# Table loads on GpSimd's DMA queue, transposes behind the first loads, the inverse p matrix in its own tile, and tasks ordered by longest path

## The chip, the cores and the metric

The kernel runs on one core of one Trainium2 chip. Time is the device time of one execution in microseconds (us). All runs of one table row come from the same chip and are compared only with runs of the kernel before made beside them.

"Slow" is a run over 1.5% above the fastest of the same kernel; ratios use fast runs alone. A ratio is the mean time of one kernel's fast runs over that of the other's fast runs of the same rounds, so it is not quite the ratio of the medians quoted beside it, which cover all runs; its 95% interval stands in brackets. "Span" is the profiled execution, some 2 us shorter than the time of a whole run. Each kernel has one profile, and its positions carry a scatter that no edit made: the first eight 128x512 matmuls of branch B took 1.89 us in the profile of the kernel before and 3.12 to 3.55 in those of b4, b6, b7 and b8, whose edits lie behind them. So a position that differs by 2 or 3 us between two profiles shows nothing by itself; ratios of times rest on several runs.

## The reference, cut to what matters

```python
def _A_ref(x, w_r, w_i):                      # spectral filter, x: 1 x 2048 x 512
    X = rfft2(x.astype(float32), axes=(-2, -1))
    X = X * (w_r + 1j * w_i)                  # w: 2048 x 257, bf16
    return irfft2(X, s=(S, D), axes=(-2, -1)).astype(bfloat16)
def _B_ref(x, w1, b1, w2):                    # 512 -> 1792 -> 512
    h = x @ w1 + b1
    sp = log1p(exp(-abs(h))) + where(h > 0, h, 0)
    return (h * tanh(sp)) @ w2
g = sigmoid((x * gate_w).sum(-1, keepdims=True))
return g * _A_ref(x, A_w_r, A_w_i) + (1 - g) * _B_ref(x, B_w1, B_b1, B_w2)
```

## The kernel before: the parts that matter

The whole program is a graph of tasks. A list scheduler, run when the kernel is built, puts every task on an engine and fixes each engine's order; the engines then run their lists with semaphores. Some tasks may go to several engines, each with an estimated time and a bias. Branch B works in four chunks of 512 rows: first matrix (`mm1`), eviction with bias (`h`), exp, ln and tanh on ScalarE, a multiply (`mul`), second matrix (`mm2`). Branch A's filter tables are loaded, moved into place in 16 pieces of 32 x 2064, and half-copied: the real part as it is, the imaginary part negated.

```python
        def dve4(n): return 0.10 + n * 0.00027          # estimates of the scheduler
        def pool(n, k=2.15): return 0.12 + n * k * 0.001
        ...
        for ri, (src, nm) in enumerate(((A_w_r, "wr"), (A_w_i, "wi"))):
            ...                                         # ten table loads, SyncE's queue
                    ld(f"{nm}{fh}s{j}", sg[pm:32:2, fs, :], wv[:, ms, :], us, cls="d_w", writes=[(nm, fh, "s", j)])
        for t in range(xtp, NT):                        # eight DMA transposes of x, same queue
            ld(f"xt{t}", xT[:, t // 4, :, t % 4, :], xv[:, t, :], 0.64, cls="d_xt", transpose=True, writes=[("xT", t)])
        ...                                             # a table move, 32 x 2064
                            if pt == 0:
                                return e.tensor_copy(out=o_, in_=i_)
                            return e.tensor_scalar(out=o_, in0=i_, scalar1=1.0, scalar2=0.0, op0=ALU.mult, op1=ALU.add)
        ...                                             # the half copy, 64 x 4160; ri == 1: negated
                def f_dup(e, ri=ri, f0=f0, dstv=dstv):
                    if ri == 0:
                        return e.tensor_copy(out=dstv[64:128, f0:f0 + 32, :], in_=dstv[0:64, f0:f0 + 32, :])
                    return e.tensor_scalar(out=dstv[0:64, f0:f0 + 32, :], in0=dstv[64:128, f0:f0 + 32, :], scalar1=-1.0, scalar2=None, op0=ALU.mult)
                G.any(f"{nm}n{fh}", [("dve", dve4(4160), f_dup), ("pool", pool(4160, 0.95), f_dup, "b_dup")], "w", ..., writes=[wk])
        ...                                             # In (the filter's input) reuses the staging tile
            dma(f"s1r{g}", rE[g:128:4, 0:8192], scr_r[...], 1.5, reads=[("scr", g)], writes=[("In", g)], deps=t_mv)
```

The two imaginary half copies are called `win0` and `win1` below, the imaginary moves `wim...`, the evictions of the third chunk `h2_...`, multiplies `mul...`, one filter product `p2_0`. An eviction copies a result of the matrix engine (PE) out of PSUM. The matmul stages of branch A are p, d and t on the way in (their evictions: `ep`, `ed`, `et`), it and id on the way back; the inverse p matrix belongs to id. The gate is 64 small matmuls on the transposes of x; a gated output is branch B's result scaled by 1 - g. `deps=t_mv` says that the filter's input is read back only when all 16 moves are done.

## Time and profile before

| | before |
|---|---|
| time, median of 3 runs | 152.81 us (152.56 to 154.8) |
| span of the profiled run | 150.9 us |
| eight multiplies of the first chunk, VectorE | 13.0 us |
| wait of the gate for the transposes, matrix engine | 2.69 us |
| the "edge" (start of the first matmul behind the last filter add) | 105.55 us |
| span behind the edge | 45.4 us |

The prediction below shows the lines behind these. Two more are needed later: how the negations ran before. Here is their row in the groups of instructions (line, engine, operation, output<-input with shapes, count | busy us, mean ns of one | idle time before):

```profile
L757 DVE TENSOR_SCALAR rA<-rA 64x4160 bf16<-64x4160 bf16 x2 | 2.5, 1240 | 0.1
```

And these are lines of VectorE's work in order (start us, length us, engine, line, operation, and in brackets the idle time before and who ended it; `...` marks lines left out):

```profile
59.21 0.17 DVE L714 CAST ezb<-ez 128x16 bf16<-128x16 f32 x1 [0.28 <-ACT ez L713]
...
60.52 3.48 DVE L922 TENSOR_TENSOR rD<-ps,b1f 128x1024 bf16<-128x1024 f32 x3
...
74.75 1.29 DVE L948 TENSOR_TENSOR hs<-hs,uT 128x1024 bf16<-128x1024 bf16 x2 [1.28 <-ACT uT L939]
```

The negations run on VectorE in 1.24 us each. A 128x16 copy takes 0.17 us, three evictions 3.48 us, two multiplies 1.29 us.

### The profile page before, as it was taken

How to read it: one execution, taken by the hardware profiler on the slowest of the kernel's cores; microseconds unless marked ns; L12 is line 12 of the kernel's file. 1: busy time of each engine (PE TensorE's matmuls, PEld its weight loads, DVE VectorE, ACT ScalarE, POOL GpSimd, SP SyncE). 2: the span in 40 equal slices, each digit the busy share in tenths (PEclk: the TensorE clock that was granted, in tenths of full speed). 3: DMA queues.
4: the chain of work that ended last, by engine and by line, in shares of the span. 5: the costliest groups of instructions: out<-in, count | busy, mean ns of one | idle time of the engine just before them, and what ended most of it. 6: DMA issues, size and time to landing. Idle time of an engine off the chain costs nothing.

```text
span 150.9 us, 2300 instructions
## 1 busy us (share of the span) xinstructions
PE 134.9 (89%) x917; PEld 72.8 (48%) x917; DVE 128.6 (85%) x150; ACT 116.3 (77%) x77; POOL 45.7 (30%) x39
## 2 busy tenths in 40 slices
PE   5697999889957988999999999896799999999992
PEld 3455555454425323444456553342256667634471
DVE  0378996969999998989698999998869979999791
ACT  3549667699997733999999999998798999971111
POOL 3000059998977994001100005951000000000000
PEclk9999999999999599999999999999689999999999
DMA  5899999998848993998004765300000000000563
GB/s 130 278 361 379 166 181 145 321 343 150 189 102 177 304 297 67 371 412 343 4 0 110 168 146 147 69 0 0 0 0 0 4 0 0 0 4 0 208 230 120
DMA packets 22686, 22.37 MB, mean 148 GB/s; under 512 B 13524, under 2 KB 19540, under 8 KB 22228
## 3 DMA queue, kind: packets, MB, share of 16 engines
q1 hardware_dynamic: 22352, 22.00, 52.6%
q10 hardware_dynamic: 324, 0.23, 0.5%
q8 instruction: 7, 0.11, 0.4%
q14 instruction: 3, 0.02, 0.1%
HBM read 14.89 MB, written 4.19 MB: 126 GB/s over the span
## 4 chain that ended last, share of the span: by engine, by line
PE 69%; DVE 19%; DMA 6%; issue 2%; ACT 2%; SPq 1%; DVEq 0%
PE ps L964 30%; PE ps L915 26%; DVE hs L948 9%; DMA w_sb<-in_B_w_dram 4%; DVE hs L922 3%; PE ps L894 3%; PE ps L855 2%; PE ps L782 2%; DMA rE<-c_inv 2%; PE ps L990 2%; PE ps L688 2%; DVE rA L559 2%; DVE rB L663 1%; DVE rW L756 1%; PE ps L677 1%
## 5 line engine op out<-in xcount | busy, mean ns | idle before, releaser
L915 PE MATMUL ps<-rX,w_sb 128*128 128x512 bf16 x224 | 52.5, 388 | 1.7 <-DVE rE L880 0.8
L964 PE MATMUL ps<-w_sb,hs 128*128 128x512 bf16 (+1 forms) x182 | 39.5, 363 | 1.5 <-DMA w_sb<-in_B_w_dram 1.0
L915 PEld LDWEIGHTS ps<-rX,w_sb 128*128 128x128 bf16 x224 | 21.7, 100 | 27.5 <-issue 2.3
L922 DVE TENSOR_TENSOR hs<-ps,b1f 128x1024 bf16<-128x1024 f32 x21 | 25.3, 1217 | 3.4 <-PE ps L915 3.2
L964 PEld LDWEIGHTS ps<-w_sb,hs 128*128 128x128 bf16 x182 | 17.3, 98 | 19.9 <-DVE hs L948 2.4
L938 ACT ACTIVATE uT<-uT 128x4096 bf16<-128x4096 bf16 (+1 forms) x8 | 25.5, 3190 | 0.2
L939 ACT ACTIVATE uT<-uT 128x4096 bf16<-128x4096 bf16 (+1 forms) x8 | 25.5, 3188 | 0.1
L948 DVE TENSOR_TENSOR hs<-hs,uT 128x1024 bf16<-128x1024 bf16 (+1 forms) x24 | 22.0, 976 | 1.3 <-ACT uT L939 1.3
L936 ACT ACTIVATE uT<-hs 128x2048 bf16<-128x2048 bf16 (+1 forms) x12 | 20.3, 1691 | 3.2 <-DVE hs L948 2.1
L964 PE MATMUL ps<-w_sb,rD 128*128 128x512 bf16 x56 | 14.9, 414 | 1.0 <-DVE rD L948 1.0
L562 ACT ACTIVATE rC<-ps 128x1024 bf16<-128x1024 f32 x14 | 14.0, 1022 | 1.7 <-PE ps L677 1.7
L978 ACT ACTIVATE rX<-ps,omg 128x512 bf16<-128x512 f32 (+1 forms) x8 | 5.3, 660 | 11.1 <-PE ps L964 11.1
L744 POOL COPY rW<-rE 32x2064 bf16<-32x2064 bf16 x4 | 7.8, 1959 | 18.6 <-DMA rE<-in_A_w_r_dram 18.3
L663 DVE TENSOR_TENSOR rB<-rA 128x1024 bf16<-128x1024 bf16 (+2 forms) x10 | 6.6, 692 | 5.5 <-DMA rA<-in_A_x_dram 5.5
L559 DVE CAST rA<-ps 128x1024 bf16<-128x1024 f32 x7 | 8.6, 1294 | 1.1 <-PE ps L894 1.1
L796 POOL TENSOR_TENSOR rC<-rC,rW 128x1024 bf16<-128x1024 bf16 x2 | 4.0, 2025 | 18.0 <-DMA tmp<-rC 18.0
L559 DVE CAST rF<-ps 128x1024 bf16<-128x1024 f32 x8 | 9.1, 1216 | 0.4 <-PE ps L855 0.4
L744 POOL COPY rA<-rE 32x2064 bf16<-32x2064 bf16 x4 | 9.3, 2319 | 0.4 <-POOL rA L733 0.3
L994 DVE SCALAR_TENSOR_TENSOR rX<-ps,gcol,rX 128x512 bf16<-128x512 f32 x12 | 8.3, 745 | 1.2 <-PE ps L990 1.1
L964 PEld LDWEIGHTS ps<-w_sb,rD 128*128 128x128 bf16 x56 | 5.5, 104 | 7.1 <-issue 1.7
L922 DVE TENSOR_TENSOR rD<-ps,b1f 128x1024 bf16<-128x1024 f32 x7 | 8.3, 1218 | 0.7 <-PE ps L915 0.7
L981 DVE TENSOR_SCALAR rX<-ps,omg 128x512 bf16<-128x512 f32 (+1 forms) x9 | 6.5, 719 | 2.0 <-PE ps L964 1.8
(79 smaller groups left out, 160.8 us busy)
## 6 DMA issues: line engine op xcount, KB each, us to landing
rF<-c_m SPq DMA_DIRECT2D x1, 2048.0 KB, 12.7
scr<-rD SPq DMA_DIRECT2D x4, 512.0 KB, 7.4
rB<-c_g SPq DMA_DIRECT2D x1, 2048.0 KB, 7.9
rE<-scr SPq DMA_DIRECT2D x4, 512.0 KB, 9.8
tmp<-rC SPq DMA_DIRECT2D x16, 128.0 KB, 2.3
out_dram<-rX SPq DMA_DIRECT2D x7, 256.0 KB, 2.0
rA<-in_A_x_dram SPq DMA_DIRECT2D x3, 512.0 KB, 10.0
w_sb<-in_B_w_dram SPq DMA_DIRECT2D x2, 768.0 KB, 9.9
```

The lines of the kernel that those rows point to most:

```text
L559: return e.tensor_copy(out=o(), in_=i())
L562: return e.activation(o(), i(), AF.Copy)
L663: return e.tensor_tensor(out=xu[:, a:b_, uv, :], in0=x_sb[:, a:b_, 0:256], in1=x_sb[:, a:b_, 256:512], op=ALU.add if uv == 0 else ALU.subt ...
L744: return e.tensor_copy(out=o_, in_=i_)
L915: ins = e.matmul(bank(b, i), w1_sb[:, dt_, 128 * ft:128 * (ft + 1)], xT[:, c, dt_, :, :], start=(dt_ == 0), stop=(dt_ == 3))
L922: return e.tensor_tensor(out=hs[hb][:, ft:ft + 2, :], in0=pair(b).rearrange("p (f s) -> p f s", f=2), in1=b1f[:, ft:ft + 2].unsqueeze(2).t ...
L936: return e.activation(o, hsf[hb][:, 512 * a:512 * b_], fn_)
L938: return e.activation(o, o, fn_, bias=1.0)
L939: return e.activation(o, o, fn_)
L948: return e.tensor_tensor(out=v, in0=v, in1=uv_[:, a:b_, 128 * tl:128 * (tl + 1)], op=ALU.mult)
L964: ins = e.matmul(bank(b)[:, 0:hi - lo], hs[hb][:, ft, 128 * tl:128 * (tl + 1)], w2_sb[:, ft, lo:hi], start=(ft == 0), stop=(ft == NFT - 1))
L994: return e.scalar_tensor_tensor(out=bs[:, t, :], in0=bank(b), scalar=gcol[:, t:t + 1], in1=bs[:, t, :], op0=ALU.mult, op1=ALU.add)
```

## The change

The intent: take loads off SyncE's queue so that the transposes come early, stop one small load from waiting for a reused tile, and let a priority by longest path (with newly searched weights) choose engines and order. The core of the diff:

```diff
-            t.prio = kn[t.cls] + t.off
+            t.prio = kn[t.cls] + t.off + (kn["bl"] * t.bl if t.cls[:2] != "f_" else 0.0)
...
-KN = dict( ... b_fil=-0.6, b_rev=20.3, b_rva=27.3, b_dup=25.7, d_w=113.1, d_xt=84.15, ...)
+KN = dict( bl=1.0, f_ld=300.0, f_xt=299.0, f_w=299.0, ... b_rev=0.19, b_rva=0.5, b_dup=-1.0, )
...
+        rft = sb("rft", [128, 128], BF)
-        RFT = cinv[:, 0, :]
+        RFT = rft[:, :]
+        dma("rft", rft[:, :], d_inv[:, 0, :], 0.3, "f_late", writes=["rft"], deps=t_p[6:7])
...
-                    ld(f"{nm}{fh}s{j}", ..., us, cls="d_w", writes=[(nm, fh, "s", j)])
+                    ld(f"{nm}{fh}s{j}", ..., us, cls="f_w", queue="pool", deps=[t_x2], writes=[(nm, fh, "s", j)])
-            ld(f"xt{t}", ..., 0.64, cls="d_xt", transpose=True, writes=[("xT", t)])
+            ld(f"xt{t}", ..., 0.64, cls="f_xt", transpose=True, nd=128, writes=[("xT", t)])
```

## The prediction

> **What bounds the kernel now.** I read the busy shares first, then the engines' busy time by stage, then the chain of work that ended last, and last the order of instructions where the chain leaves the PE.
>
> The busy shares, page part 1:
>
> ```profile
> PE 134.9 (89%) x917; PEld 72.8 (48%) x917; DVE 128.6 (85%) x150; ACT 116.3 (77%) x77; POOL 45.7 (30%) x39
> ```
>
> No engine has much room: PE stands still for 16.1 of the 151 us, DVE for 22, ACT for 35. The same by stage (columns: stretch in us, its length, busy us of PE, PEld, DVE, ACT, POOL with counts, granted PE clock, DMA share, GB/s):
>
> ```profile
> 0.00:12.00 12.00, 8.09 (x70) 5.24 (x70) 5.08 (x8) 5.74 (x8) 1.49 (x9) 1.00 0.81 265
> 12.00:44.00 32.00, 30.19 (x216) 16.46 (x216) 28.10 (x28) 26.73 (x20) 22.13 (x14) 1.00 0.99 220
> 44.00:60.00 16.00, 12.12 (x103) 5.64 (x104) 15.51 (x15) 8.86 (x6) 12.69 (x9) 0.89 0.80 207
> 60.00:76.00 16.00, 16.00 (x79) 7.37 (x77) 13.93 (x16) 15.85 (x8) 1.07 (x4) 1.00 0.65 269
> 76.00:104.00 28.00, 27.17 (x173) 13.96 (x171) 27.11 (x36) 27.74 (x20) 8.30 (x4) 1.00 0.36 86
> 104.00:112.00 8.00, 5.57 (x24) 2.25 (x24) 6.01 (x14) 6.55 (x6) 0.00 (x0) 0.79 0.00 0
> ...
> 148.00:151.00 3.00, 0.23 (x3) 0.00 (x0) 0.48 (x1) 0.00 (x0) 0.00 (x0) 1.00 0.37 124
> ```
>
> PE is idle 3.9 us in the start, 1.8 in 12 to 44, 3.9 in 44 to 60, 0.8 before 104, 2.4 in 104 to 112, 2.8 at the end. In the two stretches with clock below 1 it is also slow. The order of work shows why (start, length, engine, line):
>
> ```profile
> 15.74 5.37 SPq L523 DMA_TRANSPOSE rX<-in_A_x_dram  x1
> ...
> 22.28 14.18 SPq L523 DMA_TRANSPOSE rX<-in_A_x_dram  x2
> ...
> 45.84 13.00 DVE L948 TENSOR_TENSOR hs<-hs,uT 128x1024 bf16<-128x1024 bf16 x8
> ...
> 46.38 1.74 PE L707 MATMUL ps<-gw_sb,rX 128*128 128x1 bf16 x64 [2.69 <-DMA rX<-in_A_x_dram]
> ...
> 54.15 4.28 POOL L745 TENSOR_SCALAR rA<-rE 32x2064 bf16<-32x2064 bf16 x2
> ```
>
> The transposes sit behind ten filter-table loads and block the SP queue for 20 us, so the gate matmuls wait 2.69 us. Eight multiplies take 13.0 us while GpSimd moves filter tables until 58.4; late in the kernel four of 768 take 1.95 us and two of 1024 take 1.28, so eight should take 4.4. That is 8.6 us of DVE time lost on the path. The chain shows the third loss, the inverse matrix (start, length, what):
>
> ```profile
> 89.25 3.11 DMA rE<-c_inv
> ...
> 94.20 0.61 DVE rE L880
> ...
> 105.55 0.18 PE ps L818
> ```
>
> The load waits for the filter matmuls because it reuses their tile; a PSUM pair is held until it lands. And 105.55 is the "edge" matmul, behind the last filter add; everything after it (it, id, mm2 of chunks 2 and 3, output) takes 150.9 - 105.55 = 45.4 us.
>
> **What the Trainium skill says.** "TensorE: Matmul & The Clock Gate", Part 1: an idle window of about 3.4 us halves the PE clock and about 3.4 us of work restores it. The trace agrees: after the gate wait 20 matmuls of 512 take 6.16 us instead of 20 x 0.2165 = 4.33, after the edge 8 take 3.57 instead of 1.73; 1.8 us lost each time.
> "SBUF — State Buffer", "SBUF: two separate sides": DVE instructions with two SBUF inputs, or in a 2-port mode, and GpSimd exclude each other for a whole instruction, and a DMA queued on GpSimd has its descriptors written by GpSimd and can be starved by DVE. The trace agrees on the first (13.0 against 4.4 us); no GpSimd-queued DMA exists in it to test the second.
> "DMA: Bandwidth & Descriptors", "Issuing engines are not separate DMA queues": another queue saves issue time only, the 16 engines are shared. The DMA share of 0.99 in 12 to 44 says the same bytes will still need those engines.
>
> **The change part by part.**
> Transposes: eight of 1.5 us (the last five took 7.64) start right after the x loads. They land near 27 us, well before the gate, which now comes after all 112 mm1 matmuls of chunks 0 and 1, near 36. Won on PE: 2.7 + 1.8 throttle. The second-half weights land in the thirties, before their use after 40: the 0.74 + 0.24 + 0.51 = 1.5 us that mm2 waited for at 55 to 59 should go too.
> Inverse p matrix: the early load frees the PSUM pair. Won: 0.8 us.
> Table loads on GpSimd: SP no longer blocks, GpSimd spends perhaps 10 x 1 us issuing (an estimate: the DMA page's 1 us first byte; SP took 0.64 each). GpSimd idled 18.3 us for the tables here, so this is hidden.
> Order: this is the large part, and it moves work between engines. Counting instructions against before: DVE gets 6 table moves (estimate 1.2 us each, 2064 elements at half the rate of the 64x4160 copy that takes 1.26), 6 evictions of t instead of 0, 3 more of p, 3 more filter operations; it gives up 4 evictions of h, 4 butterfly adds, 2 half-table copies, 3 multiplies and two others. Sum: 7.2 + 6.9 + 3.6 + 1.9 + 0.8 - 4.9 - 1.8 - 2.5 - 1.5 - 1.6 = +8 us. It loses some of the collisions with GpSimd, which cost 8.6 in the multiplies alone. So DVE is about as full as before and the PE cannot simply close its gaps.
>
> DVE up to the last filter add, changed order: 24 h x 1.17 = 28.1; 5 ep x 1.20 and 5 ed x 1.29 = 12.5; 6 et x 1.15 = 6.9; 23 filter operations x 0.645 = 14.8; 13 multiplies 7.4; 6 moves 7.2; butterflies 3.6; 2 copies 2.5; 4 output scalings 3.0; small ones 0.9. Sum 86.9 us. The first h can be evicted at 9.9 (w1 lands at 8.0, eight matmuls 1.7); butterflies of 1.0 precede. DVE is then bound by PE until chunk 1's last h: PE reaches the stream of 104 mm1 matmuls at about 11.4 and needs 104 x 0.2165 = 22.6, so 34; h ends at 35.2, DVE having 21.4 us of work in 25.3, idle 3.9. So with no collision: 9.9 + 85.9 + 3.9 + 0.5 = 100. Collisions remain: GpSimd's nine moves of 1.95 us run from about 24 to 43, over five butterflies or moves and the first two or three multiplies, 1 to 1.5 us each; estimate 4 to 6 in all. The edge then comes at 104 to 106, against 105.55.
> The same walk for the filter input: the last DVE table move ends at 59 (no collision) to 64, the scratch is read back in 8 (before: 59.5 to about 71 with 2 MB of G in front, now behind), the first t at 69 to 73; before 76.05. From there DVE has about 31 us of work to the edge and PE 29.6.
> After the edge: the 45.4 us of before minus throttle 1.8 if the gap is shorter, minus small waits: 43.5 to 45. Chunk 3's exp also hangs on the edge (its buffer is freed by chunk 2's multiplies), so ACT does not pull ahead there.
> Sum: 100 + 44 = 144 at best, 105.5 + 45 = 150.5 as I expect collisions; the runs are 1.9 us longer than the span (152.81 against 150.9).
>
> **The rivals.**
> 1. PE rules: the removed waits (2.7 + 1.8 + 1.5 + 0.8 = 6.8) come off whole: 146. For it: PE's share is the highest, and the order was plainly chosen anew so that collisions fit. Against it: DVE at 27.11 of 28 us before the edge.
> 2. DVE rules: gains of the first half are spent at six moves and six evictions: about 152. For it the sum above; against it, GpSimd is free of table moves 15 us earlier.
> 3. GpSimd's descriptor writing is starved or slower than 1 us each: bf4 on GpSimd, queued behind ten issues, delays p4 past 34 us, and PE idles and cools: 155 or more. No line speaks for or against it; GpSimd has 34 - 9.4 = 24 us for 10 issues and two adds of 2, so each issue may take 2 us before it hurts.
>
> **How the range follows.** Between rival 1 (146) and the walk (152) I take 149.6, since my walk adds up waits that an order sought by machine can partly step around. Low 145.5 is the collision-free walk, high 154 the walk with rival 3 at work a little. Faster by over 2% means below 149.75: 0.49; within 2%: 0.43; slower: 0.08.
>
> **What would show it.** Right: no wait of the gate for a transpose; full clock at 44 to 60; the rE<-c_inv wait gone from the chain; eight chunk-0 multiplies in 5 to 9 us; first t at 69 to 73; edge at 102 to 106. Wrong: moves on DVE of 2 us instead of 1.2 (then a wait of PE for h near 65), a PE wait for p4 near 34 (rival 3), or an edge before 100, which would mean collisions vanished and rival 1 holds.

## The result, and the profile after

| | before, beside it | after |
|---|---|---|
| time, median of 4 runs | 153.81 us (152.56 to 156.99) | 170.55 us (165.26 to 176.01) |
| ratio of fast runs | | 1.080 (1.059 to 1.102) |
| span of the profiled run (fast) | 150.9 us | 164.4 us |
| edge | 105.55 us | 119.46 us |
| span behind the edge | 45.4 us | 44.9 us |

Two of the four runs of the changed kernel are fast (166.13 and 165.26), and the ratio rests on them. In the profiles everything is lost ahead of the edge: 13.9 us, and 0.4 won behind it. The edge after, and the busy shares:

```profile
119.46 0.18 PE L844 MATMUL ps<-rC,rD 128*128 128x1 bf16 x1 [1.53 <-DVE rC L828]
```

```profile
PE 137.3 (84%) x902; PEld 75.5 (46%) x917; DVE 135.8 (83%) x154; ACT 116.5 (71%) x78; POOL 62.0 (38%) x48
```

GpSimd (POOL) has 16 us more to do, VectorE (DVE) 7 us more although it gave work away. By stage (columns as in the prediction's table of stages):

```profile
34.00:48.00 14.00, 8.61 (x127) 6.97 (x126) 8.99 (x8) 13.91 (x7) 13.26 (x7) 0.76 1.01 240
...
76.00:104.00 28.00, 20.80 (x132) 10.96 (x132) 28.00 (x22) 18.45 (x14) 24.92 (x10) 0.94 0.21 56
```

In 34 to 48 the matrix engine is idle for 5.4 us and its clock falls to 0.76; I come back to that. In 76 to 104 VectorE counts as busy all the time but does only 22 instructions (36 before in the same stretch), GpSimd is busy 24.9 us instead of 8.3, and the matrix engine idles 7.2 us. So look at what GpSimd does there, in the order of its work:

```profile
70.37 10.74 POOL L782 TENSOR_SCALAR rA<-rA 64x4160 bf16<-64x4160 bf16 x1
...
81.92 5.72 POOL L974 TENSOR_TENSOR hs<-hs,uT 128x768 bf16<-128x768 bf16 x3
...
89.77 10.92 POOL L782 TENSOR_SCALAR rA<-rA 64x4160 bf16<-64x4160 bf16 x1
```

And at VectorE at the same times:

```profile
60.40 0.70 DVE L770 TENSOR_SCALAR rA<-rE 32x2064 bf16<-32x2064 bf16 x1
...
69.66 4.62 DVE L948 TENSOR_TENSOR rD<-ps,b1f 128x1024 bf16<-128x1024 f32 x4
74.19 6.21 DVE L974 TENSOR_TENSOR hs<-hs,uT 128x1024 bf16<-128x1024 bf16 x2
...
82.59 3.56 DVE L974 TENSOR_TENSOR hs<-hs,uT 128x1024 bf16<-128x1024 bf16 x2
...
94.08 5.89 DVE L825 TENSOR_TENSOR tmp<-tmp,rA 128x1024 bf16<-128x1024 bf16 x2
```

Each negation takes 10.8 us on GpSimd, against 1.24 on VectorE. VectorE's pair of multiplies that meets the first takes 6.21 us instead of 1.29, and ends at 80.4; the pair of filter products that meets the second takes 5.89 instead of about 1.3, and ends just under 100. The recorded ends of the negations are 81.1 and 100.7, so these came free some 0.7 us or more before the recorded end (the page calls GpSimd's spans rough). The four evictions from PSUM at 69.66, which overlap the first negation, take their usual 1.15 us each. A busy VectorE here is a VectorE that stands still. The two stalls are 4.9 + 4.6 = 9.5 us. The pair at 82.59 (3.56) and the one at 88.33 (1.77 for one) are long as well; they stand beside GpSimd's three multiplies, not beside a negation, and are not in this sum.

The other reading is in the start: SyncE's queue (SPq), and the gate on the matrix engine, with a second wait of the matrix engine that section 4 takes up:

```profile
6.11 33.26 SPq L545 DMA_TRANSPOSE rX<-in_A_x_dram  x8
```

```profile
40.91 1.84 PE L732 MATMUL ps<-gw_sb,rX 128*128 128x1 bf16 x64 [4.33 <-DMA rX<-in_A_x_dram]
...
70.94 5.35 PE L941 MATMUL ps<-rX,w_sb 128*128 128x512 bf16 x23 [2.08 <-DVE rD L948]
```

The transposes do start at 6 us, but issuing the eight takes until 39.4, and the gate waits 4.3 us for them instead of 2.7. The wait for the p matrix is gone from the chain of waits.

### The profile page after: what moved, and what is told of

The parts are those of the page before. It is cut to its first block, busy times and chain, and to the rows that moved or that the text cites.

```text
span 164.4 us, 2288 instructions
## 1 busy us (share of the span) xinstructions
PE 137.3 (84%) x902; PEld 75.5 (46%) x917; DVE 135.8 (83%) x154; ACT 116.5 (71%) x78; POOL 62.0 (38%) x48
## 4 chain that ended last, share of the span: by engine, by line
DVE 33%; SPq 23%; PE 21%; ACT 11%; issue 5%; DMA 4%; DVEq 0%; ACTq 0%
SPq L545 19%; PE ps L990 13%; DVE hs L974 8%; DVE tmp L825 5%; DVE rC L583 5%; ACT uT L962 4%; SPq L546 4%; ACT uT L964 4%; DVE rD L948 3%; DVE rC L828 3%; DMA tmp<-rC 2%; DVE rC L822 2%; PE ps L713 2%; DMA rX<-in_A_x_dram 2%; PE ps L1016 2%
## 5 line engine op out<-in xcount | busy, mean ns | idle before, releaser
L948 DVE TENSOR_TENSOR hs<-ps,b1f 128x1024 bf16<-128x1024 f32 x19 | 22.6, 1217 | 6.3 <-PE ps L941 6.1
L782 POOL TENSOR_SCALAR rA<-rA 64x4160 bf16<-64x4160 bf16 x2 | 21.7, 10830 | 0.2
L583 DVE CAST rC<-ps 128x1024 bf16<-128x1024 f32 x11 | 12.9, 1212 | 4.9 <-PE ps L702 4.9
L990 PE MATMUL ps<-w_sb,rD 128*128 128x512 bf16 x53 | 12.6, 379 | 0.5 <-DVE tmp L855 0.4
L1004 ACT ACTIVATE rX<-ps,omg 128x512 bf16<-128x512 f32 x7 | 4.8, 685 | 9.0 <-PE ps L990 9.0
L586 ACT ACTIVATE rC<-ps 128x1024 bf16<-128x1024 f32 x5 | 5.0, 1014 | 6.9 <-PE ps L808 6.9
L688 DVE TENSOR_TENSOR rB<-rA 128x1024 bf16<-128x1024 bf16 (+1 forms) x6 | 4.8, 842 | 5.7 <-DMA rA<-in_A_x_dram 5.7
L825 DVE TENSOR_TENSOR tmp<-tmp,rA 128x1024 bf16<-128x1024 bf16 x7 | 9.2, 1339 | 0.0
L769 POOL COPY rW<-rE 32x2064 bf16<-32x2064 bf16 x3 | 5.7, 1897 | 8.8 <-DMA rE<-in_A_w_r_dram 8.8
L920 PE MATMUL ps<-rE,rF 128*128 128x256 bf16 x64 | 7.8, 273 | 1.2 <-ACT rA L586 0.8
```

The lines of the kernel that those rows point to most:

```text
L583: return e.tensor_copy(out=o(), in_=i())
L825: return e.tensor_tensor(out=zv(z), in0=zv(z), in1=Wi[:, fa:fb, 0:128], op=ALU.mult)
L948: return e.tensor_tensor(out=hs[hb][:, ft:ft + 2, :], in0=pair(b).rearrange("p (f s) -> p f s", f=2), in1=b1f[:, ft:ft + 2].unsqueeze(2).t ...
L990: ins = e.matmul(bank(b)[:, 0:hi - lo], hs[hb][:, ft, 128 * tl:128 * (tl + 1)], w2_sb[:, ft, lo:hi], start=(ft == 0), stop=(ft == NFT - 1))
```

## The experiments

Theory A: the negations on GpSimd shut VectorE out for most of their 10.8 us. Theory C: table loads on GpSimd's queue and transposes slow one another. Theory O: VectorE's new order costs. The rival to A throughout: the new order, not the negations, is at fault.

Nearly all edits leave the scheduler's result alone and then move single tasks in the finished lists, with this hook. An edit below is its list: (task, new engine, task behind which it goes).

```diff
         G.schedule(KN)
+        _repin(G)      # moves the tasks of REPIN in g.order; adds the waits of EXTRA
```

### 1. The negations alone (b4_neg_pool, e1_win_dve)

The kernel before, with the negations alone moved to GpSimd:

```diff
+REPIN = [('win0', 'pool', 'wim111'), ('win1', 'pool', 'wiz0')]
+EXTRA = [('win0', ['wim111']), ('win1', ['wiz0'])]
```

> The kernel before with the third part alone: the two half-table negations go from VectorE to GpSimd, right after its last table moves; nothing else is moved. If they are what costs most in the changed kernel (theory A), each takes 10.5 to 11 us on GpSimd here too, from about 58 to 80 us, a pair of VectorE's bf16 multiplies between 70 and 80 us takes 3 us or more in place of 1.29, and the span is 154 to 159 us. If the cause is elsewhere, VectorE is 2.5 us lighter and the span is 148 to 151 us.

Measured: 166.01 us median (164.8 to 167.09) against 153.8, ratio 1.080 (1.074 to 1.087), span 165.0. One moved pair of tasks, out of the whole change, costs what the whole change costs. GpSimd and VectorE in this run:

```profile
61.47 10.91 POOL L757 TENSOR_SCALAR rA<-rA 64x4160 bf16<-64x4160 bf16 x1
...
73.13 10.73 POOL L757 TENSOR_SCALAR rA<-rA 64x4160 bf16<-64x4160 bf16 x1
```

```profile
62.16 10.26 DVE L714 CAST ezb<-ez 128x16 bf16<-128x16 f32 x1 [0.28 <-ACT ez L713]
...
73.50 3.48 DVE L922 TENSOR_TENSOR rD<-ps,b1f 128x1024 bf16<-128x1024 f32 x3
...
79.55 2.47 DVE L718 TENSOR_TENSOR gcol<-ez,omg 128x16 f32<-128x16 f32 x1
```

The 128x16 copy, 0.17 us before, starts just behind the negation and ends at 72.42; the negation ends at 72.38. Its own work is nothing; it is held to the end of the other engine's instruction, as closely as the records tell. While the second negation runs, three evictions that read PSUM take 3.48 us, exactly as before: they are not held. A 128x16 multiply that reads SBUF alone is: 2.47 us at 79.55, where it took 0.17 before. Its end, 82.02, is 1.8 us ahead of the recorded end of the negation (83.86), so "held to the end" is exact for the copy only. The two stalls, 10.1 + 2.3 = 12.4 us, are about what the medians differ by (12.2). The expectation missed which instruction would be hit (I named the multiplies at 70 to 80 us); the first gate instruction was, and the matrix engine then waited 8.0 us in one piece for the third chunk's evictions. The edge came at 120.50, 15 us later than before; some 3 of these stood already at 48.79, where the first chunk's multiplies begin (45.84 before), ahead of both negations, so they are not their doing.

The changed kernel, with the negations alone moved back:

```diff
+REPIN = [('win0', 'dve', 'h2_0'), ('win1', 'dve', 'o4_0')]
```

> The changed kernel with its two half-table negations (64x4160) on DVE instead of GpSimd, all else in place. Theory A, the negations (10.7 and 10.9 us on GpSimd) shut DVE's two-input instructions out: the two multiplies that took 6.2 us and the two filter products that took 5.9 fall to 1.3 each, DVE gains 9.5 us and pays 2 x 1.26 for the copies, and a throttled stretch goes: span 164.4 falls by 8 to 11, to 153 to 156. Rival B, the late transposes and tables set the time: the gain is under 4 us, span above 160.

Measured: 160.89 us median (159.26 to 167.16) against 153.94, ratio 1.034 (1.028 to 1.040), span 157.4, edge 112.06. The edge is 7.4 us earlier than in the changed kernel, a little less than I gave A. The negations are over half of the loss, and something else holds the rest.

### 2. Is it the duration? (e2_win_2op, b5_neg_2op)

The table moves are written with two operations; the negation with one. The same for the negation, still on GpSimd:

```diff
-scalar1=-1.0, scalar2=None, op0=ALU.mult)
+scalar1=-1.0, scalar2=0.0, op0=ALU.mult, op1=ALU.add)
```

> The changed kernel with the negation kept on GpSimd but written as multiply and add (two operations, as the table moves are), same result. If the single-operation form is what makes it 2.6 ns an element (the moves take 0.92), it falls to about 4 us and the span by 5 to 7. If the element count, the 64 partitions or the shift of partitions make it slow, it stays at 10 to 11 us and the span at 164.

In the groups of the changed kernel, then of this run:

```profile
L782 POOL TENSOR_SCALAR rA<-rA 64x4160 bf16<-64x4160 bf16 x2 | 21.7, 10830 | 0.2
```

```profile
L782 POOL TENSOR_SCALAR rA<-rA 64x4160 bf16<-64x4160 bf16 x2 | 7.3, 3654 | 0.2
```

The same 64x4160 negation takes 3.65 us. Time: 163.75 us median (159.84 to 168.21); three of the four runs, the profiled one too, were slow, so there is no ratio and I draw nothing from the time. The two-operation form in the kernel before (the edit of b4_neg_pool plus this one):

> The kernel before with its two half-table negations on GpSimd as in the run that cost 8.0%, but written with two operations (times -1, plus 0). If the harm comes from how long one such instruction holds GpSimd's and VectorE's way to SBUF (10.8 us each in the one-operation form), it shrinks with the duration: 3.65 us each, no small VectorE instruction of 128x16 over 4 us, and, as GpSimd is idle here from 58 us on and VectorE gives up 2 x 1.24 us, a span of 149 to 153 us. If any move of this work to GpSimd is bad, or the harm came from the order, the span stays above 158 us.

Measured: 158.77 us median (155.85 to 159.09) against 155.31 on a restless chip, three of four slow, so again no ratio; the one fast run (155.85) lies well below b4_neg_pool's fastest (164.8), but outside the range that I had written. The instruction lengths in the profile do not hang on that:

```profile
62.20 3.18 DVE L714 CAST ezb<-ez 128x16 bf16<-128x16 f32 x1 [0.28 <-ACT ez L713]
```

The same copy is held 3.2 us instead of 10.3, again to the end of a negation (61.51 + 3.84 = 65.35). So the stall of this copy is as long as what is left of GpSimd's instruction. VectorE's freed 2.5 us did not make the time better than before in any run.

### 3. Loads and transposes (e3_tab_sp, e4_xt_wait, b2_xt_first, b3_tab_pool)

The changed kernel with the table loads back on SyncE's queue, behind the transposes (`TAB` stands for the ten loads, each behind the one before):

```diff
+REPIN = [(TAB[0], 'sp', 'xt15'), ..., (TAB[9], 'sp', TAB[8])]
```

> The changed kernel with the ten table loads back on the SP queue, behind the eight transposes. Theory C, table packets of the GpSimd queue slow the transposes that run beside them: each transpose issues in about 1.3 us once the x loads are through, the last lands by 24 us instead of 40.8, the gate's 4.3 us wait and the half-rate clock behind it (40 to 48 us) go; tables land around 30 to 36 as now; span 158 to 161. Rival D, the transposes are slow by themselves behind the loads: the last still lands after 35 us and the span stays near 164 or rises, since the tables come later still.

Measured: 166.11 us median (164.69 to 167.0), ratio 1.080 (1.074 to 1.086), span 162.7.

```profile
6.10 14.37 SPq L545 DMA_TRANSPOSE rX<-in_A_x_dram  x8
```

```profile
45.85 3.05 PE L990 MATMUL ps<-w_sb,hs 128*128 128x512 bf16 x7 [3.29 <-DVE hs L974]
```

Without those loads beside them the eight take 14.4 us to issue, not 33.3, and the gate does not wait at all. Yet the time is that of the changed kernel: the matrix engine now waits 3.3 us for VectorE's first-chunk multiplies a little later, and the negations follow as before.

The reverse, the first transpose made to wait for all ten table loads on GpSimd's queue:

```diff
+EXTRA = [('xt8', TAB)]
```

> The changed kernel with the first transpose waiting until all ten tables (GpSimd queue) have landed. Theory C: the tables land much earlier than 35 us (near 22) because no transposes run beside them, the transposes then take 1.3 us each and land by 34 to 36, the gate waits little; span 158 to 162. Rival D: tables land at 30 or later all the same, transposes land after 42, span 166 or more.

Measured: 165.15 us median (163.51 to 165.69), ratio 1.070 (1.062 to 1.077). The loads landed 9.3 to 13.6 us after issue, where they took 13.5 to 22.5 beside the transposes in the changed kernel. Against the expectation the gate now waited 5.28 us for the late transposes, but these took:

```profile
28.66 10.46 SPq L545 DMA_TRANSPOSE rX<-in_A_x_dram  x8
```

Half of theory C is shown: the eight transposes take 33.3 us to issue beside the ten loads, 14.4 without them beside and 10.5 behind them. The other half is not: in f1_tab_kept (section 4), with both together, the loads landed in 9.4 to 14.4 us, as in e4_xt_wait. Nor is it shown that GpSimd's queue matters: in the kernel before, all on SyncE's queue, the first three transposes, issued while other loads were under way, took 5.37 + 14.18 us, and the last five 7.64. The cost in time is open too: each way out ends in the next wait.

The kernel before with each part alone. First the transposes behind the first loads, tables behind them, all on SyncE's queue:

```diff
+REPIN = [('xt8', 'sp', 'x4'), ('xt9', 'sp', 'xt8'), ..., ('xt15', 'sp', 'xt14')]
```

> The kernel before with one part of the change alone: its eight transposes are moved on SyncE's queue to right behind the first loads of x, and the table loads follow behind them on the same queue. My prediction's first term says that this alone removes the gate's wait for the transposes (2.7 us) and the low clock behind it (1.8 us): span 146.5 to 149 us. Rival: the tables come some 10 us later, GpSimd's eight or so table moves run later and stand against VectorE's multiplies of the first chunk, and what is won at the gate is given back: edge at 105 us or later, span 150 to 153 us.

Measured: 156.65 us median (155.97 to 157.88) against 153.8, ratio 1.021 (1.015 to 1.027). GpSimd and VectorE:

```profile
28.18 4.21 POOL L744 COPY rW<-rE 32x2064 bf16<-32x2064 bf16 x2 [25.85 <-DMA rE<-in_A_w_r_dram]
```

```profile
48.81 12.94 DVE L948 TENSOR_TENSOR hs<-hs,uT 128x1024 bf16<-128x1024 bf16 x8
```

The gate no longer waits, but the table moves start 7.6 us later (20.6 before), run on until 65.5 (58.4 before), and VectorE's multiplies beside them still take 12.94 us and end 3 us later than before (61.7 against 58.8). Of these 3 us, 1.6 stood already at 39.32 (37.69 before) and may be the scatter of the start, and 1.3 came from a half copy on VectorE that met GpSimd's moves (2.90 us at 40.58, 1.29 before). That fits the rival that I had written, but does not show it: a loss of 2.1% is what the times show, a longer collision of 1.3 us is what one profile shows.

Then the ten loads alone on GpSimd's queue:

```diff
+REPIN = [(TAB[0], 'pool', 'wrp1'), ..., (TAB[9], 'pool', TAB[8])]
+EXTRA = [(TAB[0], ['x2'])]
```

> The kernel before with another part alone: the ten table loads are issued from GpSimd's queue, right after its first two memsets, with nothing else moved. If loads on that queue and transposes slow one another (theory C), the eight transposes take over 20 us here from first issue to last landing and the tables land over 9 us after issue, and the gate waits as long as before or longer: span 151 to 156 us. If the queue is harmless (what I predicted), the transposes start some 6 us earlier on SyncE and land by 31 us, the gate does not wait, and the span is 147 to 150 us.

Measured: 154.75 us median (153.94 to 157.64), ratio 1.0045 (0.9996 to 1.0094), span 153.8.

```profile
15.07 24.96 SPq L523 DMA_TRANSPOSE rX<-in_A_x_dram  x2
```

```profile
50.22 1.84 PE L707 MATMUL ps<-gw_sb,rX 128*128 128x1 bf16 x64 [3.96 <-DMA rX<-in_A_x_dram]
```

Two transposes hold SyncE's queue for 25 us (14.2 before), and the gate waits 4.0 us. Slow transposes again, at a price of about half a per cent (at most 0.9 by the interval).

### 4. What holds the rest (e5_win_tab, e7_mul_dve, e8_h2_first, e9_h2_gap, f1_tab_kept)

The edits of e1_win_dve and e3_tab_sp together:

> The changed kernel with two parts undone at once: the two half-table negations back on VectorE, and the table loads back on SyncE's queue right behind the transposes. The new order of tasks, the own tile of the inverse p matrix and the transposes right behind the first loads stay. If the two causes are separate (each alone gave 7 us and about 0 us, the second because the 10.8 us negations stood behind it), they now add up: gate wait 0, no VectorE multiply pair over 4 us from 70 to 90 us, the edge at 106 to 109 us and a span of 151 to 154 us, level with before within 2%. If the new order of tasks itself costs (the GpSimd multiplies and the late gate evictions of the slow path), the edge stays at 110 us or later and the span at 155 us or more, 3% or more above before.

Measured: 159.97 us median (158.77 to 160.91), all fast, ratio 1.041 (1.035 to 1.047), span 158.0. They do not add up; the order itself costs. VectorE and the matrix engine:

```profile
67.96 0.75 DVE L1007 TENSOR_SCALAR rX<-ps,omg 128x512 bf16<-128x512 f32 x1 [2.54 <-PE ps L990]
68.74 1.24 DVE L781 COPY rW<-rW 64x4160 bf16<-64x4160 bf16 x1
70.01 1.23 DVE L948 TENSOR_TENSOR rD<-ps,b1f 128x1024 bf16<-128x1024 f32 x1
```

```profile
71.29 7.04 PE L941 MATMUL ps<-rX,w_sb 128*128 128x512 bf16 x23 [2.08 <-DVE rD L948]
```

VectorE evicts the third chunk's first pair at 70.01 (60.52 before), behind a gated output for which it waits 2.54 us, and the matrix engine waits 2.08 us for that eviction. Two suspects: GpSimd's three multiplies and one filter product (76 to 87 us), and this order. First the multiplies, on top of e5_win_tab:

```diff
+REPIN += [('mul1_1_0', 'dve', 'et3'), ('mul1_1_1', 'dve', 'mul1_1_0'),
+          ('mul1_1_3', 'dve', 'mul1_1_2'), ('p2_0', 'dve', 'win1')]
```

> The changed kernel with negations and table loads undone (which left it 4.1% above before) and, besides, GpSimd's three multiplies and one filter product of 76 to 87 us given back to VectorE: none of the order of the others changes. If these multiplies hold VectorE up as the table moves did, the pair that took 4.03 us takes 1.3 us again and the edge comes 2 to 3 us earlier, at 110 to 111 us, span 155 to 156 us, for VectorE takes 2.6 us of their work on itself. If they were free, VectorE's extra work makes it 2 us slower, span 159 to 161 us.

Measured: 159.47 us median (156.8 to 159.55) against 155.31, three of four runs slow, no ratio: inconclusive in time. The multiplies that took 4.03 us in e5_win_tab take 1.28 (in the profiled, slow run). Then, on top of that, three evictions ahead of VectorE's table moves:

```diff
+REPIN += [('h2_0', 'dve', 'o1_0'), ('h2_2', 'dve', 'h2_0'), ('h2_4', 'dve', 'h2_2')]
```

> As the run before it, and VectorE takes the first three evictions of the third chunk (ready near 60 us) right after its first two gated outputs, ahead of five table moves and two copies, where the kernel before has them too. In the run without the negations and with the loads back, the first of them ran at 70.0 us against 60.5 us in the kernel before, though the gate was 4 us earlier there. If this order is what still costs, the matrix engine's wait of 2.1 us at 71 us goes and the edge comes 2 to 4 us earlier than without it, span 151 to 154 us. If the moves and copies only wait elsewhere then, the edge moves by under 1 us.

Here "the run before it" is e7_mul_dve. Measured: 162.59 us median (160.76 to 164.8), ratio 1.052 (1.033 to 1.072). A miss, and two lines say why:

```profile
62.94 3.49 DVE L948 TENSOR_TENSOR rD<-ps,b1f 128x1024 bf16<-128x1024 f32 x3 [3.15 <-DMA scr<-rD]
```

```profile
78.74 0.88 PE L808 MATMUL ps<-rE,rF 128*128 128x128 bf16 x8 [5.18 <-DMA rE<-scr]
```

The eviction writes a buffer that a DMA still reads until 62.9, so VectorE stood still 3.15 us; and the table moves, pushed back, held up the read of the filter's input (`deps=t_mv`), for which the matrix engine then waited 5.18 us. So the evictions go behind the moves and one copy, but ahead of the gated output:

```diff
-REPIN += [('h2_0', 'dve', 'o1_0'), ('h2_2', 'dve', 'h2_0'), ('h2_4', 'dve', 'h2_2')]
+REPIN += [('h2_0', 'dve', 'wrn0'), ('h2_2', 'dve', 'h2_0'), ('h2_4', 'dve', 'h2_2')]
```

> The changed kernel with negations and loads undone and GpSimd's multiplies on VectorE, as twice before, and the first three evictions of the third chunk on VectorE after its five table moves and the first copy, ahead of the gated output that it waited 2.6 us for. Ahead of the moves they cost time (they waited 3.15 us for a read of the buffer that they write, and the reads of the scratch buffer came 5.2 us late, span 158.8 us); here the buffer is free (from 62.9 us on) and the moves are done. If VectorE's order between the gate and the third chunk is the rest of the loss, the matrix engine's wait of 2.1 us at 70 us is gone and the edge is at 108 to 109.5 us against 111.1 us, span 153.5 to 155.5 us. If the matrix engine's own order (28 products of the second matrix ahead of the third chunk) bounds it, the edge stays within 0.7 us of 111.1 us.

Measured: 155.34 us median (154.54 to 156.83), all fast, against 154.15, ratio 1.010 (1.003 to 1.017), span 152.7.

```profile
64.70 3.49 DVE L948 TENSOR_TENSOR rD<-ps,b1f 128x1024 bf16<-128x1024 f32 x3
...
72.55 1.28 DVE L974 TENSOR_TENSOR hs<-hs,uT 128x1024 bf16<-128x1024 bf16 x2
```

The evictions run at 64.70, the wait of the matrix engine near 70 us is gone, and the edge is at 107.85. From e5_win_tab's 112.98 that is 5.1 us for the multiplies and the order of three evictions together; the runs do not split it cleanly, as e7_mul_dve was slow. Of the changed kernel's +8.0% one per cent is left, and it stays open.

Last, e9_h2_gap with the table loads kept on GpSimd's queue (the edit of e9_h2_gap without `TAB`):

> As the run before it (1.010 of before), but the ten table loads stay on GpSimd's queue as in the change: the one part whose cost no run has shown free of the negations' stalls. If the race of these loads with the transposes costs on the path, the gate waits 2 to 5 us for the last transposes again, the edge comes at 109 to 112 us against 107.9 us, and the ratio is 1.015 to 1.04. If the wait that it makes is hidden behind VectorE's multiplies of the first chunk, which end at 50 us in any case, the ratio stays at 1.005 to 1.015.

Measured: 159.32 us median (153.99 to 166.83), four of six runs slow, no ratio. The profiled run is fast, span 153.6, edge 108.71: the gate did not wait, though the eight transposes took 26.9 us to issue (14.65 in e9_h2_gap, without those loads). So the queue need not cost anything on the path, but the runs spread over 12.8 us where e9_h2_gap's spread over 2.3. There is a pattern in this: of the kernels with the changed order, those with the loads beside the transposes spread over 7.9 to 12.8 us (the changed kernel, e1, e2, f1), and those with the two apart over 2.1 to 4.0 (e3, e4, e5, e7, e8, e9), with four to six runs each. Why some runs are so long no fast run shows; left open.

### 5. The inverse p matrix alone, and a better kernel (b1_rft, b6_wim_off, b7_wim_dve, b8_wim_rft)

The kernel before with the matrix in a tile of its own, and its users' wait changed to that load, every engine's order kept:

```diff
+        rft = sb("rft", [128, 128], BF)
-        RFT = cinv[:, 0, :]
+        RFT = rft[:, :]
+        dma("rft", rft[:, :], d_inv[:, 0, :], 0.3, ..., writes=["rft"], deps=t_p[6:7])
+REPIN = [('rft', 'sp', 'ldM')]
```

> The kernel before with the last part of the change alone: the inverse p matrix in a tile of its own, loaded early, with every engine's order kept. I had put its gain at 0.8 us (the wait for this load in the chain). If that holds, the span is 150 to 150.6 us, ratio 0.990 to 0.998, and the load is gone from the chain of waits. If VectorE's order, which stays as it is, is what sets that stretch, the time is the same within 0.3%.

Measured: 154.27 us median of 22 runs against 154.15, ratio 1.0025 (0.9995 to 1.0055). The load is gone from the chain of waits and nothing is won. The profiles show what stands there instead: a filter add on VectorE (2.42 us at 91.18 in the kernel before, 2.44 at 92.81 here, where its neighbours take 0.69) beside a filter product on GpSimd, one more collision that moving the load does not touch.

The lesson of sections 1 and 3, used on the kernel before: take GpSimd's last four moves away from the multiplies. First two on ScalarE and two late on VectorE:

```diff
+REPIN = [('wim110', 'act', 'exp1_4'), ('wim111', 'act', 'wim110'),
+         ('wim100', 'dve', 'h2_8'), ('wim101', 'dve', 'wim100')]
```

> The kernel before with four of GpSimd's table moves (those at 49 to 58 us, which stand against VectorE's eight multiplies of the first chunk) taken off it: two on ScalarE, where it waited idle near 54 us, two on VectorE at about 67 us. The eight multiplies took 13.0 us against about 5.2 us alone; with four of the moves gone they should take 6 to 9 us, the small gate instructions come 4 us or more earlier, and after 1.4 us for VectorE's two moves and the next wait for the second matrix's load the span falls to 147 to 150 us. Rival: another wait (that load, or the tanh chain of ScalarE that the two moves push back) takes its place, and the span stays at 150 to 153 us.

Measured: 155.17 us median of 20 runs against 155.31, ratio 1.001 (0.997 to 1.005). VectorE (from a profiled run that was slow; the lengths of instructions are what I read here):

```profile
47.64 6.16 DVE L948 TENSOR_TENSOR hs<-hs,uT 128x1024 bf16<-128x1024 bf16 x8
...
59.99 0.18 DVE L714 CAST ezb<-ez 128x16 bf16<-128x16 f32 x1 [6.11 <-ACT ez L713]
```

The multiplies fall from 13.0 to 6.16 us, and VectorE then waits 6.11 us for ScalarE's exponential of the gate, which stands behind the two moves there. The rival held: a new wait took the place of the old one. So the four go to VectorE, into that very gap:

```diff
+REPIN = [('wim100', 'dve', 'zcl'), ('wim101', 'dve', 'wim100'),
+         ('wim110', 'dve', 'wim101'), ('wim111', 'dve', 'wim110')]
```

> The kernel before with GpSimd's last four table moves given to VectorE, right after its first-chunk multiplies and the copy of the gate's sums, where it waited for the second matrix product. In the run with two on ScalarE and two late on VectorE the eight multiplies fell from 13.0 to 6.16 us, but two other waits ate it: ScalarE's small exponential of the gate stood behind its two moves (6.1 us) and the reads of the scratch buffer stood behind VectorE's late moves (2.3 us on the matrix engine). Here neither should come: moves done by 57 us, first eviction of the third chunk at 57 to 59 us in place of 60.5, edge at 102.5 to 104.5 us, span 148 to 150 us, ratio 0.98 to 0.993. If the wait for the second matrix's load takes all of it, the time is the same within 0.5%.

Measured: 151.95 us median (149.51 to 152.91) against 154.15 (152.92 to 157.88), ratio 0.978 (0.971 to 0.985) from three fast runs of six. VectorE in its profiled run, which was slow (152.28), so that again only lengths are read:

```profile
47.42 6.17 DVE L948 TENSOR_TENSOR hs<-hs,uT 128x1024 bf16<-128x1024 bf16 x8
53.51 0.16 DVE L711 TENSOR_SCALAR zcl<-ps 128x16 f32<-128x16 f32 x1
53.70 1.44 DVE L744 COPY rA<-rE 32x2064 bf16<-32x2064 bf16 x2
55.18 1.44 DVE L745 TENSOR_SCALAR rA<-rE 32x2064 bf16<-32x2064 bf16 x2
```

Four moves that cost GpSimd 8.9 us and VectorE some 7 us of stalls cost VectorE 2.9 us. In that slow profile the first eviction of the third chunk (59.45) and the edge (105.12) came later than expected. With the p matrix's own tile added:

> Both of the runs before it at once, as a candidate to beat the kernel before: if their gains add up, a span of 147.5 to 149.5 us and a ratio of 0.975 to 0.99; if the matrix's load bounds both, the same as the second of them alone.

"The runs before it" are b1_rft and b7_wim_dve. Measured: 151.78 us median (150.78 to 153.03), all six fast, ratio 0.986 (0.981 to 0.992). The two are one result within their spread: the six runs of b7_wim_dve, slow ones too, average 151.5 us, those of b8_wim_rft 151.8. The safer figure is the 1.4% of b8_wim_rft, whose runs are all fast; the 2.2% leans on the three fast runs that a single 149.51 left. Both are gains over the kernel before, which is the faster of the two kernels. No gain of the tile shows.

## Why the prediction was wrong

The step that failed is in "Order": VectorE "gives up ... 2 half-table copies", booked as -2.5 us and never charged to GpSimd. On GpSimd they take 10.83 us each, and the collisions that the prediction allowed for ("GpSimd's nine moves of 1.95 us", "estimate 4 to 6 in all") left them out. Measured in their place: 9.5 us of stalls of VectorE in the changed kernel, 7.4 us of the edge when they are undone, and 8.0% when they are the only thing done (b4_neg_pool). I quoted the exclusion between the two engines and then did not ask, for each instruction that moved, how long it would hold the other engine. No row of the profile before had this form on GpSimd; that should have been a rival, and none of the three named it. The scheduler made the same error with its estimate of 4.07 us, which fits the two-operation form (3.65) and not this one.

The other steps:

- Transposes "of 1.5 us each", landing near 27: wrong beside the table loads. Issuing the eight took until 39.4 us, and the gate waited 4.33 us. The size would have been nearly right without them (14.4 us for eight). The prediction's own lines held the warning: the three transposes that shared the time with other loads had taken 5.37 + 14.18 us, and it reckoned with the last five alone. "Won on PE: 2.7 + 1.8 throttle" was also wrong as a gain: alone, with the table loads behind them, the early transposes made the kernel before 2.1% slower.
- The clock: the slow matmuls after a wait are there (6.16 us instead of 4.33), but the quoted window of about 3.4 us of idleness is not in these lines: the idle time ahead of them was 2.69 us, and after the edge 1.45 and 0.99, each with small matmuls between.
- "Inverse p matrix ... Won: 0.8 us": the wait went from the chain as predicted, the gain was 0 (1.0025).
- "GpSimd spends perhaps 10 x 1 us issuing": 5.8 us for ten, less than estimated. "Hidden": alone in the kernel before nearly so, at 0.45%. Rival 3 feared the matrix engine near 34 us; instead the transposes were slowed.
- Moves on VectorE "estimate 1.2 us each": 0.70 us (60.40). The term was too large, not too small.
- "Eight chunk-0 multiplies in 5 to 9 us": right, they took 5.6 us (six 4.61, two 0.99).
- First t "at 69 to 73": its matmul came at 76.13, as late as before (76.05). The walk hung it on the read of the filter's input; the trace hangs it on the third chunk. In the changed kernel it follows that chunk's 23 products at once, and these had waited 2.08 us for the late evictions at 69.66. With these at 64.70 (e9_h2_gap, which also differs in the negations, loads and multiplies) it came at 73.57; without the negations, but with late evictions (e5_win_tab), at 78.17. The walk added up VectorE's work without its wait for the gated output ahead of those evictions: undoing that and GpSimd's multiplies moved the edge by 5.1 us.
- Edge "at 102 to 106": 119.46. After the edge "43.5 to 45": 44.9, right.
- The 0.92 given to "within 2%" or better rested on no stall longer than a table move. With the negations' 9.5 us of stalls added, the prediction's own sum of 150.5 + 1.9 becomes 161.9 (an estimate); the 3.4 us left up to the fastest run (165.3) are less than the 5.1 us that section 4 found in the order.

## What to carry to other kernels

Before work moves to GpSimd, ask how long one instruction there takes in exactly its form, and which VectorE instructions that work in SBUF alone fall into that time: here such ones were held to about its end, however small they were themselves (evictions from PSUM were not), and the profile then shows a busy VectorE. Read every changed weight of a scheduler as a change of the program: here the move of two tasks, which the description did not mention, cost the kernel before as much as the whole change. And put work that collides where the other engine waits anyway, as the four moves in b7_wim_dve; freeing an engine at a place that is followed by another wait (b2_xt_first, e3_tab_sp, b6_wim_off) won nothing in these runs.

## What the Trainium skill lacked or had wrong

- "GPSIMD Engine Reference", 4.1 Engine selection, says that one-input elementwise work on GpSimd "is roughly line-rate". The runs show two rates for the same negation of 64x4160 bf16: 10.83 us (2.6 ns per element of a partition) with one operation, 3.65 us (0.88 ns) with a second, idle one. The page does not tell them apart.
- "SBUF — State Buffer", "SBUF: two separate sides", says that whichever of the two engines starts first keeps the shared pair for the whole instruction. The runs agree, and add the size of the worst case seen: a 128x16 copy of 0.17 us took 10.26 us, up to the end of the negation, while evictions that read PSUM ran at their usual 1.16 us each. VectorE's instructions with two inputs came free 0.7 to 1.8 us before the recorded end of GpSimd's instruction; as GpSimd's spans are rough, that is no contradiction shown.
- "DMA: Bandwidth & Descriptors", Rules for kernel authors, says that a transpose next to ordinary DMAs "needs nothing". That sentence is about waits that keep the data right, and there the runs agree (all results were right). What the page lacks is the time a transpose takes beside other loads: eight transposes took 26.9 to 36.7 us to issue beside ten loads on GpSimd's queue, 13.8 to 15.7 with those loads behind them on one queue, 10.5 behind the loads. The loads were slower beside them in some kernels (13.5 to 22.5 us to land) and not in another (9.4 to 14.4, against 9.3 to 13.6 apart). Whether starved descriptor writing, the shared DMA engines or something else is the cause no run here shows.
